# One attention-and-FFN decode step on one core: a TensorE loop over one pair of batches instead of two, with V copied to a fixed place

## The chip, the core and the metric

The kernel runs on one core of one Trainium2 chip. Five engines work side by side, each on its own instruction stream, and meet only at semaphores: TensorE (PE in the profile) multiplies matrices and writes to the accumulator banks (PSUM), VectorE (DVE) and ScalarE (ACT) read those banks and write to on-chip memory (SBUF), GpSimd (POOL) fills and copies SBUF, SyncE (SP) starts nearly all transfers. Transfers from main memory are carried out by 16 DMA engines that all transfers share. The metric is device time in microseconds (us) for one execution; lower is better.

## What is computed

One new token for each of four batches goes through layer normalisation, and its result through two branches whose outputs are added to the input: attention over a window of 4096 cached positions (32 query heads, 8 kv heads, head size 128) and a SwiGLU FFN of width 1792. Cut to what matters:

```python
x = A_x                                   # (4, 1, 512)
xn = _layernorm(x, axis=-1)
def _A_ref(x, k_cache, v_cache, wq, wo):  # caches (4, 8, 16384, 128)
    q = (x @ wq).reshape(B, 1, 32, 128).transpose(0, 2, 1, 3)
    k = jnp.repeat(k_cache[:, :, Sk - W:, :], 4, axis=1)   # W = 4096
    v = jnp.repeat(v_cache[:, :, Sk - W:, :], 4, axis=1)
    p = _softmax(jnp.einsum("bhqd,bhkd->bhqk", q, k) * (128 ** -0.5), axis=-1)
    o = jnp.einsum("bhqk,bhkd->bhqd", p, v)
    return o.transpose(0, 2, 1, 3).reshape(B, 1, 32 * 128) @ wo
def _B_ref(x, w_gate, w_up, w_down):
    return (_silu(x @ w_gate) * (x @ w_up)) @ w_down
return x + _A_ref(xn, ...) + _B_ref(xn, ...)
```

Everything is bf16 in memory. The K and V windows are 64 MB of the 81 MB that are read.

## The kernel before

**The unit of work** is a turn: one kv head of two batches. There are ND = 16 of them. A turn's K is one load of 2048 KB to `KB[128, 8192]`, its V one load to `VB`, each with two buffers; positions and the two batches lie on the 128 partitions, so a mask takes out the scores of the wrong batch. A turn is cut in halves of 32 blocks of 128 positions.

**What happens to a turn's data**: TensorE transposes 32 blocks of K (`transposes`, line 397) into four accumulator banks of 8 blocks each (groups g = 0 to 3), the four banks are copied to `KT` in SBUF (`evac`, L311, all by VectorE), and 32 score matmuls (`scores`, through the helper at L369) multiply `KT` by the queries of the turn; then the same for the second half. Scores of both halves fill one bank `ps_S`. VectorE takes their maximum along the free axis (`row_max`, L316), TensorE turns it over the partitions (`max_rows`), VectorE reduces it and makes a diagonal `Dg` (`shift`, L321 to L323), TensorE subtracts it from all scores by a matmul (`shift`), ScalarE takes exp into `P` (L282). Then TensorE sums the denominators (4 matmuls with `ones`) and multiplies `P` by V (`pv`, 32 matmuls a half), and VectorE normalises into `OT` (`norm`, L327 to L331).

**Order.** The stages of neighbouring turns overlap. TensorE's stream is written by hand: in each pass of its loop (L445) two turns, b = 0 and 1, and in each turn d: transposes of the first half, maximum of the scores of d - 1, second half of PV of d - 2, mask and scores of the first half, shift of d - 1, transposes of the second half, denominators and first half of PV of d - 1, scores of the second half. For this the scores have two banks, `P` two halves, and the queries of the turn are read from `QZ` at an address taken from a register (`QF[:, ds(...)]`), since one pass of the loop names only b. Every wait is a `wait_ge` on a semaphore, in a loop against a value computed from the loop register.

**Transfers** are started by SP in the order of its stream: WQ at the start, then K of turns 0 and 1, gate and up weights, V of turn 0, then K(d) and V(d - 1) by turns; the down weights stand before the last V, and the five pieces of WO at the end. K(d) waits until K(d - 2) has been transposed, V(d) until the PV of d - 2 is done.

**Around the loop**: layer normalisation and the query projection before it, with `QZ` filled at L302; after it the gate and up projections (from L466), the last PV, the down projection, four transposes of `OT`, a regrouping, and the rows of WO (`out_rows`, L193), then y and its store. ScalarE loads its function table three times: before L273, L277 (square root) and L282 (exp).

Of the kernel before, what the change touches and what calls it, by code (L numbers as in the profile page):

```python
# [5 lines left out]
BF16 = mybir.dt.bfloat16  # L6
FP32 = mybir.dt.float32
# [5 lines left out]
def bass_parallel_sum__sliding_block_cached__swiglu_ffn__decode_kernel(  # L13
# [72 lines left out]
    OT = sb("oT", [128, B, REP + HQ], BF16)  # L86
# [13 lines left out]
    ps_S = [ps("ps_s%d" % s, [128, 512], FP32) for s in range(2)]  # L100
# [8 lines left out]
    mt_ps = ps_acc[0:C, 0:128]  # L109
# [29 lines left out]
    s_tr = sem("s_tr")  # L139
    s_ev = sem("s_ev")  # L140
# [28 lines left out]
    def kv_ap(cache, d, fold):  # L169
        b0 = d % 2 * 2  # L170
        return cache[b0:b0 + 2, d // 2, Sk - W:, :].rearrange("b (q t) d -> q b (t d)", t=fold * NT)
# [13 lines left out]
    def load_kv(eng, buf, cache, d):  # L185
        return load(eng, buf[:, d % 2 * KVN:(d % 2 + 1) * KVN], kv_ap(cache, d, 1), kv_ap(cache, d, FOLD))
# [10 lines left out]
    with nc.Block() as block:  # L197

        @block.gpsimd
        def _(eng):  # L200
# [32 lines left out]
            eng.memset(VB[:, HKN:].bitcast(FP32), 0.0)  # L233
            eng.drain()
            eng.engine_nop().then_inc(s_const, 1)
            eng.engine_nop().then_inc(d_v[1], 16)
# [33 lines left out]
        def _(eng):  # L270
# [9 lines left out]
            for d in range(-1, ND):  # L280
                eng.wait_ge(s_sh, d + 2)
                eng.activation(P[:, d % 2 * PS:d % 2 * PS + SN], ps_S[d % 2][:], ACT.Exp, scale=SCALE).then_inc(s_p, 1)  # L282
# [4 lines left out]
        def _(eng):  # L287
# [13 lines left out]
            for i in range(2):  # L301
                last = eng.tensor_copy(  # L302
                    QZ[:].rearrange("p (k i) c -> p k i c", i=2)[:, :, i, 0:C].rearrange("p k (m h) -> p k m h", m=2),
                    qT.rearrange("p (k h x) -> p k x h", h=REP, x=32)[:, :, 2 * i:2 * i + 2, :])
            last.then_inc(s_qz, 1)
            eng.engine_nop().then_inc(s_ev, NG)

            def evac(u, tr):
                for g in range(NG):
                    eng.wait_ge(s_tr, tr + g + 1)  # L310
                    eng.tensor_copy(KT[:, u * HKN + 1024 * g:u * HKN + 1024 * (g + 1)],  # L311
                                    kt_ps[g].rearrange("p a b -> p (a b)")).then_inc(s_ev, 1)

            def row_max(bank, n):
                eng.wait_ge(s_sc, n)
                eng.tensor_reduce(RM[:], ps_S[bank][:].rearrange("p (t c) -> p c t", c=C), AX.X,  # L316
                                  ALU.max).then_inc(s_rm, 1)

            def shift(n):
                eng.wait_ge(s_mt, n)  # L320
                eng.tensor_reduce(m8[:], mt_ps, AX.X, ALU.max)  # L321
                eng.drain()
                eng.tensor_scalar(Dg[:], I8[:], m8[:, 0:1], -1.0, ALU.mult, ALU.mult).then_inc(s_dg, 1)  # L323

            def norm(n, b, r):
# [5 lines left out]
                eng.tensor_tensor(OT[:, 2 * b:2 * b + 2, ds(r * REP, REP)],  # L331
                                  O_ps.rearrange("p (j h) -> p j h", j=2),
                                  den[:].rearrange("p (j h) -> p j h", j=2), ALU.mult).then_inc(s_nrm, 1)

            with eng.Fori(0, ND // 2) as r:
                for b in range(2):
                    row_max(1 - b, 2 * r + (b + 1))
                    evac(0, 4 * NG * r + 2 * NG * b)
                    shift(2 * r + (b + 1))
                    norm(2 * r + (b + 1), b, r)  # L340
                    evac(1, 4 * NG * r + (2 * NG * b + NG))
            row_max(1, ND + 1)
            shift(ND + 1)
            norm(ND + 1, 0, ND // 2)

# [13 lines left out]
            norm(ND + 2, 1, ND // 2)  # L359

# [6 lines left out]
        def _(eng):  # L367
# [20 lines left out]
            def mask(bank):  # L388
                return mm(ps_S[bank][:].rearrange("p (t c) -> p t c", c=C), mkr[:],
                          mkc[:].rearrange("j (o c) -> j o c", o=1).to_broadcast([2, NT, C]), start=True)  # L390

            def transposes(s, ev, b):
                for g in range(NG):
                    eng.wait_ge(s_ev, ev + g + 1)
                    for k in range(8):
                        a = b * KVN + s * HKN + 128 * (8 * g + k)
                        last = eng.transpose(kt_ps[g][:, k, :], KB[:, a:a + 128], ident[:])  # L397
                    last.then_inc(s_tr, 1)

            def scores(s, ev, b, q):  # L400
                if s == 0:
                    mask(b)
                eng.wait_ge(s_ev, ev + 2 * NG)
                for t in range(HT):
                    o = C * (s * HT + t)
                    n = min(WIDE, SN - o)
                    last = mm(ps_S[b][:, o:o + n], KT[:, s * HKN + 128 * t:s * HKN + 128 * (t + 1)], q(n))
                if s == 1:
                    last.then_inc(s_sc, 1)
# [131 lines left out]
```

## Time and profile before

| | us |
|---|---|
| three runs | 197.21, 196.9, 195.21 |
| median | 196.9 |
| span of the profiled execution | 194.3 |
| TensorE matmul, busy in the span | 164.1 |
| TensorE weight load, busy | 142.1 |
| VectorE, busy | 115.4 |
| ScalarE, busy | 17.0 |
| GpSimd, busy | 10.5 |
| read from main memory | 81.01 MB, 417 GB/s over the span |

The span runs from the first to the last instruction of one execution that the hardware profiler recorded; the device time of a run also has what lies around it, here 196.9 - 194.3 = 2.6 us by the median. In lines of a timeline the first number is the start in us from the span's start, the second the duration of the whole group, then engine, source line, operation, output <- input, and the number of instructions; brackets give the idle time of the engine before it and what ended it. In lines of a group the numbers behind the bar are busy us and mean ns of one instruction. In the chain of waits each line is start, duration and what the end of the kernel was waiting for at that time. A line that starts with SPq or ACTq is the start of a transfer.

### The profile page before, as it was taken

The page shows a single profiled execution, that of the slowest core. Times are in us where ns is not written, and L with a number is a line of the kernel's source. Part 1 is how long each engine was busy: PE and PEld are TensorE (multiplying, and loading weights), DVE is VectorE, ACT ScalarE, POOL GpSimd, SP SyncE. Part 2 cuts the span into 40 slices and gives each one's busy share as a digit, 9 for nine tenths or more (in the row PEclk, how much of TensorE's full clock was granted, in tenths as well). Part 3 has the DMA queues.
Part 4 walks back from the last instruction along what each step waited for, and adds up shares of the span by engine and source line. Part 5 has one row for each costly group of instructions (what it writes and reads, how often), then busy time and mean ns, then how long its engine had stood idle before and what let it go on. Part 6 is the DMA issues. An engine that isn't in the chain of part 4 may idle for free.

```text
span 194.3 us, 7749 instructions
## 1 busy us (share of the span) xinstructions
PE 164.1 (84%) x3460; PEld 142.1 (73%) x3461; DVE 115.4 (59%) x250; ACT 17.0 (9%) x27; POOL 10.5 (5%) x23
## 2 busy tenths in 40 slices
PE   0127999949999989898989898989898989898894
PEld 0112988848989878888878887888887888887662
DVE  1004757617677767676767676767676767675530
ACT  5700010100110101010101010101010101010100
POOL 8930000000000000000000000000000000000000
PEclk9999999988999999999999999999999999999999
DMA  6999997999999999999999999999999999999992
GB/s 217 432 432 432 511 452 332 432 437 432 425 432 425 432 432 432 438 445 432 432 432 432 438 432 438 432 438 432 432 432 432 445 432 432 432 428 428 401 400 94
DMA packets 3589, 81.09 MB, mean 417 GB/s; under 512 B 664, under 2 KB 800, under 8 KB 1184
## 3 DMA queue, kind: packets, MB, share of 16 engines
q1 hardware_dynamic: 3568, 81.01, 97.3%
q8 instruction: 4, 0.07, 0.1%
q10 hardware_dynamic: 16, 0.01, 0.0%
q14 instruction: 1, 0.01, 0.0%
HBM read 81.01 MB, written 0.00 MB: 417 GB/s over the span
## 4 chain that ended last, share of the span: by engine, by line
DMA 61%; PE 34%; issue 1%; DVE 1%; SPq 1%; DVEq 0%
DMA kbuf<-in_A_k_cache_dram 46%; PE ps_kt L397 18%; DMA wo_sb<-in_A_wo_dram 9%; PE ps_s L369 8%; DMA wq_sb<-in_A_wq_dram 6%; PE ps_o L369 5%; PE ps_kt L369 2%; PE ps_acc L369 1%; PE ps_acc L193 1%; DVE kT L311 1%; SPq L251 1%; DVE kT L299 0%; SPq L177 0%; DVE y_sb L507 0%; DVE qz L302 0%
## 5 line engine op out<-in xcount | busy, mean ns | idle before, releaser
L311 DVE COPY kT<-ps_kt 128x1024 bf16<-128x1024 bf16 x128 | 79.9, 683 | 27.4 <-PE ps_kt L397 27.3
L397 PE MATMUL ps_kt<-ident,kbuf 128*128 128x128 bf16 x1024 | 65.7, 225 | 10.4 <-DMA kbuf<-in_A_k_cache_dram 10.4
L397 PEld LDWEIGHTS ps_kt<-ident,kbuf 128*128 128x128 bf16 x1024 | 60.1, 101 | 15.8 <-issue 15.8
L369 PE MATMUL ps_o<-p,vbuf 128*128 128x64 bf16 x1120 | 39.2, 195 | 0.0
L369 PEld LDWEIGHTS ps_o<-p,vbuf 128*128 128x128 bf16 x1120 | 36.0, 99 | 1.2
L369 PEld LDWEIGHTS ps_s<-qz,kT 128*128 128x128 bf16 x1024 | 31.4, 98 | 6.7 <-issue 3.7
L369 PE MATMUL ps_s<-qz,kT 128*128 x1024 | 34.7, 192 | 1.2
L282 ACT ACTIVATE p<-ps_s 128x512 bf16<-128x512 f32 x17 | 10.2, 597 | 161.9 <-PE ps_s L369 161.9
L316 DVE TENSOR_REDUCE rm<-ps_s 128x8 bf16<-128x512 f32 x17 | 11.8, 691 | 19.8 <-PE ps_s L369 19.8
L369 PE MATMUL ps_o<-p,ones 128*128 128x128 bf16 (+1 forms) x69 | 7.0, 222 | 2.3 <-DVE qz L302 1.3
L369 PE MATMUL ps_kt<-wq_sb,xnT 128*32 128x512 bf16 x32 | 3.6, 629 | 5.3 <-DMA wq_sb<-in_A_wq_dram 5.3
L369 PEld LDWEIGHTS ps_o<-p,ones 128*128 128x128 bf16 x69 | 4.5, 98 | 3.5 <-issue 2.2
L369 PE MATMUL ps_s<-mkc,mkr 2*128 2x512 bf16 x17 | 6.9, 404 | 0.0
L374 PE MATMUL ps_acc<-i,xn 4*128 4x4 f32 x4 | 0.6, 254 | 7.4 <-ACT xn L279 7.4
L369 PE MATMUL ps_s<-dg,ones 8*128 8x512 bf16 x17 | 6.5, 385 | 0.0
L327 DVE TENSOR_REDUCE den<-ps_o 128x8 f32<-128x128 f32 x18 | 5.0, 275 | 2.5 <-PE ps_o L369 2.5
L369 PEld LDWEIGHTS ps_kt<-wq_sb,xnT 128*32 128x32 bf16 x32 | 1.2, 138 | 6.8 <-issue 6.8
L299 DVE STREAM_TRANSPOSE kT<-ps_kt 128x512 f32<-128x512 f32 x2 | 1.4, 717 | 8.0 <-PE ps_kt L369 8.0
L374 PEld LDWEIGHTS ps_acc<-i,xn 4*128 4x128 f32 x4 | 0.6, 207 | 7.3 <-issue 7.3
L233 POOL MEMSET vbuf<- 128x6144 f32 x1 | 5.2, 5222 | 0.0
L321 DVE TENSOR_REDUCE m<-ps_acc 8x1 f32<-8x128 f32 x17 | 4.6, 270 | 0.3 <-PE ps_acc L369 0.3
L331 DVE TENSOR_TENSOR oT<-ps_o,den 128x8 f32 (+1 forms) x18 | 3.0, 166 | 2.9 <-issue 2.7
(68 smaller groups left out, 48.6 us busy)
## 6 DMA issues: line engine op xcount, KB each, us to landing
kbuf<-in_A_k_cache_dram SPq DMA_DIRECT2D x16, 2048.0 KB, 12.5
vbuf<-in_A_v_cache_dram SPq DMA_DIRECT2D x16, 2048.0 KB, 11.2
wq_sb<-in_A_wq_dram SPq DMA_DIRECT2D x1, 4096.0 KB, 12.3
wo_sb<-in_A_wo_dram SPq DMA_DIRECT2D x1, 2048.0 KB, 14.9
wg_sb<-in_B_w_gate_dram SPq DMA_DIRECT2D x1, 1792.0 KB, 24.2
wu_sb<-in_B_w_up_dram SPq DMA_DIRECT2D x1, 1792.0 KB, 27.6
wd_sb<-in_B_w_down_dram SPq DMA_DIRECT2D x1, 1792.0 KB, 14.9
wo_sb<-in_A_wo_dram SPq DMA_DIRECT2D x1, 896.0 KB, 17.8
```

Source lines behind the costliest of these rows:

```text
L193: last = eng.matmul(ps_acc[64 * n:64 * n + B, 0:256], OP[:, c, :], WO[:, c, 256 * n:256 * n + 256], start=False, stop=True, skip_group_che ...
L233: eng.memset(VB[:, HKN:].bitcast(FP32), 0.0)
L251: eng.dma_start(WO[:, a:b, :], wo_ap[:, a:b, :]).then_inc(d_wo[n], 16)
L282: eng.activation(P[:, d % 2 * PS:d % 2 * PS + SN], ps_S[d % 2][:], ACT.Exp, scale=SCALE).then_inc(s_p, 1)
L299: eng.transpose(qT[:, 512 * n:512 * n + 512], ps_kt[n][:])
L311: eng.tensor_copy(KT[:, u * HKN + 1024 * g:u * HKN + 1024 * (g + 1)], kt_ps[g].rearrange("p a b -> p (a b)")).then_inc(s_ev, 1)
L316: eng.tensor_reduce(RM[:], ps_S[bank][:].rearrange("p (t c) -> p c t", c=C), AX.X, ALU.max).then_inc(s_rm, 1)
L321: eng.tensor_reduce(m8[:], mt_ps, AX.X, ALU.max)
L327: eng.tensor_reduce(den[:], den_ps.rearrange("p (t c) -> p c t", c=C), AX.X, ALU.add)
L331: eng.tensor_tensor(OT[:, 2 * b:2 * b + 2, ds(r * REP, REP)], O_ps.rearrange("p (j h) -> p j h", j=2), den[:].rearrange("p (j h) -> p j h" ...
L369: return eng.matmul(o, l, r, start=start, stop=stop, skip_group_check=True)
L397: last = eng.transpose(kt_ps[g][:, k, :], KB[:, a:a + 128], ident[:])
```

## The change

TensorE's loop now covers one turn, with static addresses, and everything that differed between turns is brought to one place:

- **V** is copied by VectorE from its buffer to `VS`, the last 8192 columns of the query weights' place, the second half of the old turn's V early in a turn and the first half of the new one's late. PV reads `VS`. V's buffer is free when its second half has been copied, and V(d) waits for that.
- **Queries**: GpSimd copies the turn's queries from `QZ` to a slot `QS`. GpSimd also waits for the landing of K and V and tells the others by `s_k` and `s_v`.
- **One score bank** and one `P`. The mask of the new scores waits until exp has read the old ones. The maximum's matmul gets a bank of its own, `ps_mt`.
- **TensorE's stream**: maximum of the last scores, transposes of the first half, shift, transposes of the second half, mask, scores of the first half, denominators, first half of PV, scores of the second half, second half of PV; the PV of a turn follows its scores by one turn. K still has two buffers, so the two transposes are written twice (`pe_even`, `pe_odd`), the rest once (`pe_both`), with branches between. The branch with a hint at the old end is gone.
- **Evacuation**: VectorE copies groups 0 and 2 of `KT`, ScalarE groups 1 and 3, exp between the halves.
- **Transfers**: K and V alternate from the start; gate, up and down weights and WO come after the last V.
- Turns run head by head over one pair of batches and then the other, and `OT` is laid out to fit.

The diff, cut to its core:

```diff
-    P = sb("p", [128, 2 * PS], BF16)
+    VS = WQ[:, NC * HQ * Dh - KVN:NC * HQ * Dh]
+    P = sb("p", [128, PS], BF16)
+    QS = sb("qs", [128, WIDE], BF16)
-    ps_S = [ps("ps_s%d" % s, [128, 512], FP32) for s in range(2)]
+    ps_S = ps("ps_s", [128, 512], FP32)
+    ps_mt = ps("ps_mt", [128, 512], FP32)
...
+    def at(d):
+        return (d + 1) % 2 * KVN
...
         @block.gpsimd
...
+            eng.wait_ge(s_qz, 1)
+            for d in range(ND):
+                eng.wait_ge(d_k[d % 2], 16 * (d // 2 + 1))
+                eng.engine_nop().then_inc(s_k, 1)
+                if d:
+                    eng.wait_ge(s_sc, d)
+                eng.tensor_copy(QS[:], QZ[:, d, :]).then_inc(s_qs, 1)
+                eng.wait_ge(d_v[d % 2], 16 * (d // 2 + 1))
+                eng.engine_nop().then_inc(s_v, 1)
...
         @block.sync
...
                 if d >= 2:
-                    eng.wait_ge(s_tr, 2 * NG * (d - 1))
+                    eng.wait_ge(s_t[1][NG - 1], d - 1)
...
-                eng.wait_ge(s_pv, d + 1)
+                if d >= 1:
+                    eng.wait_ge(s_vs[1], d)
...
-            load_k(0)
-            load_k(1)
+            for d in range(ND):
+                load_k(d)
+                load_v(d)
             load(eng, WG[:], wg_ap, fold_rows(B_w_gate)).then_inc(d_wg, 16)
             load(eng, WU[:], wu_ap, fold_rows(B_w_up)).then_inc(d_wu, 16)
-            load_v(0)
-            for d in range(2, ND):
-                load_k(d)
-                load_v(d - 1)
             load(eng, WD[:], wd_ap, fold_rows(B_w_down)).then_inc(d_wd, 16)
-            load_v(ND - 1)
...
         @block.scalar
...
-            for d in range(-1, ND):
-                eng.wait_ge(s_sh, d + 2)
-                eng.activation(P[:, d % 2 * PS:d % 2 * PS + SN], ps_S[d % 2][:], ACT.Exp, scale=SCALE).then_inc(s_p, 1)
+            with eng.Fori(1, ND + 2) as r:
+                for h in range(2):
+                    for g in (1, 3):
+                        eng.wait_ge(s_t[h][g], r)
+                        eng.activation(KT[:, h * HKN + 1024 * g:h * HKN + 1024 * (g + 1)],
+                                       kt_ps[g].rearrange("p a b -> p (a b)"), ACT.Copy).then_inc(s_e[h][g], 1)
+                    if h == 0:
+                        eng.wait_ge(s_sh, r)
+                        eng.activation(P[:, 0:SN], ps_S[:], ACT.Exp, scale=SCALE).then_inc(s_p, 1)
...
         @block.vector
...
+            with eng.Fori(1, ND + 2) as r:
+                here = eng.snap((r % 2) * KVN, min_val=0, max_val=KVN)
+                other = eng.snap(((r + 1) % 2) * KVN, min_val=0, max_val=KVN)
+                eng.wait_ge(s_mt, r)
+                eng.tensor_reduce(m8[:], mt_ps, AX.X, ALU.max)
+                eng.drain()
+                eng.tensor_scalar(Dg[:], I8[:], m8[:, 0:1], -1.0, ALU.mult, ALU.mult).then_inc(s_dg, 1)
+                norm(r)
+                for h in range(2):
+                    for g in (0, 2):
+                        eng.wait_ge(s_t[h][g], r)
+                        eng.tensor_copy(KT[:, h * HKN + 1024 * g:h * HKN + 1024 * (g + 1)],
+                                        kt_ps[g].rearrange("p a b -> p (a b)")).then_inc(s_e[h][g], 1)
+                eng.tensor_copy(VS[:, HKN:], VB[:, ds(other + HKN, HKN)]).then_inc(s_vs[1], 1)
+                eng.wait_ge(s_v, r)
+                eng.wait_ge(s_pv0, r)
+                eng.tensor_copy(VS[:, 0:HKN], VB[:, ds(here, HKN)]).then_inc(s_vs[0], 1)
+                eng.wait_ge(s_sc, r)
+                eng.tensor_reduce(RM[:], ps_S[:].rearrange("p (t c) -> p c t", c=C), AX.X, ALU.max).then_inc(s_rm, 1)
+            norm(ND + 2)
...
         @block.tensor
...
+            def turn(d):
+                r = eng.snap(count, min_val=1, max_val=ND + 1)
+                eng.wait_ge(s_rm, r)
+                mm(mt_ps, RM[:], ident[:], start=True).then_inc(s_mt, 1)
+                eng.wait_ge(s_k, r)
+                transposes(0, r, d)
+                eng.wait_ge(s_dg, r)
+                mm(St, ones[0:C, :], Dg[:].rearrange("j (o c) -> j o c", o=1).to_broadcast([C, NT, C])).then_inc(s_sh, 1)
+                transposes(1, r, d)
+
+            eng.br("pe_even")
+            with nc.body("pe_even", valid_engines=PE):
+                turn(0)
+                eng.br("pe_both")
+            with nc.body("pe_both", valid_engines=PE):
+                r = eng.snap(count, min_val=1, max_val=ND + 1)
+                eng.wait_ge(s_p, r)
+                mask()
+                eng.wait_ge(s_qs, r)
+                scores(0)
+                eng.wait_ge(s_nrm, r)
+                for j in range(SN // 128):
+                    mm(den_ps, ones[:], P[:, 128 * j:128 * (j + 1)], start=(j == 0))
+                eng.wait_ge(s_vs[0], r)
+                pv(0).then_inc(s_pv0, 1)
+                for g in range(NG):
+                    eng.wait_ge(s_e[1][g], r)
+                scores(1).then_inc(s_sc, 1)
+                eng.reg_alu(count, count, 1, ALU.add)
+                eng.reg_alu(odd, 1, odd, ALU.subtract)
+                eng.wait_ge(s_vs[1], r)
+                pv(1).then_inc(s_pv, 1)
+                eng.br_lt(odd, 1, on_true="pe_even", on_false="pe_more")
+            with nc.body("pe_more", valid_engines=PE):
+                eng.br_lt(count, ND + 2, on_true="pe_odd", on_false="pe_done")
+            with nc.body("pe_odd", valid_engines=PE):
+                turn(1)
+                eng.br("pe_both")
+            nc.switch_bb("pe_done")
...
-            eng.br_lt(flag, 1, on_true="tensor_tail", on_false="tensor_never")
-            with nc.body("tensor_never", valid_engines=[mybir.EngineType.PE]):
-                eng.br_lt(flag, 1, on_true="tensor_never", on_false="tensor_tail").branch_hint(hint)
-            nc.switch_bb("tensor_tail")
```

In the tail, the down projection now follows the transposes of `OT`, and the last PV and normalisation stand inside the loop's last turn.

More of the change, by code (lines that the diff above doesn't have):

```diff
@@ L108, in bass_parallel_sum__sliding_block_cached__swiglu_ffn__decode_kernel @@
     xT_ps = ps_acc[:, 0:NC * B]
[L109 removed]
+    mt_ps = ps_mt[0:C, 0:128]
     gate_ps = ps_kt[0][:, 0:NF * 32]
@@ L386, in _, with mask @@
                 last.then_inc(s_q, 1)
[L388 to L392, printed above, removed]
+            St = ps_S[:].rearrange("p (t c) -> p t c", c=C)
+            def mask():
+                return mm(St, mkr[:], mkc[:].rearrange("j (o c) -> j o c", o=1).to_broadcast([2, NT, C]), start=True)
@@ L411, in max_rows @@
[L411 to L433 removed]
+                    last = mm(ps_S[:, o:o + n], KT[:, h * HKN + 128 * t:h * HKN + 128 * (t + 1)], QS[:, 0:n])
@@ L481, in _ @@
                     mm(ps_acc[64 * n:64 * n + B, 0:256], guT[:, t, :], WD[:, t, 256 * n:256 * n + 256])
-            eng.wait_ge(s_nrm, ND + 2)
-            for i in range(B):
-                last = eng.transpose(
-                    tr_ps[:, i, :],
-                    OT[:, i, REP:], ident[:])
-            last.then_inc(s_t4, 1)
             spin(2)
```

141 lines of the change are left out of this document (46 added, 95 removed).

## The prediction

> **What bounds the kernel now.** I read the slices of the page first, then the chain that ended last, then the timeline of one turn (one batch pair and one kv head: K transposed, scores, exp, PV), last the DMA by stretch.
>
> ```profile
> PE   0127999949999989898989898989898989898894
> DMA  6999997999999999999999999999999999999992
> ```
>
> Two resources look full. The chain of waits tells which one ends last:
>
> ```profile
> 0.80 12.35 DMA wq_sb<-in_A_wq_dram
> ...
> 28.36 14.14 DMA kbuf<-in_A_k_cache_dram
> ...
> 78.42 12.51 DMA kbuf<-in_A_k_cache_dram
> ...
> 97.79 12.52 DMA kbuf<-in_A_k_cache_dram
> ...
> 155.97 12.52 DMA kbuf<-in_A_k_cache_dram
> ...
> 173.47 17.78 DMA wo_sb<-in_A_wo_dram
> 191.25 0.04 issue
> 191.30 1.30 PE ps_acc L193 x20
> 192.60 0.02 issue
> 192.62 0.41 DVE y_sb L507
> ```
>
> K loads land at 78.42 + 12.51 = 90.93 and two turns later at 97.79 + 12.52 = 110.31: 19.38 us for two K and two V loads, so 9.69 us a turn, 4.85 us a load of 2048 KB.
>
> ```profile
> kbuf<-in_A_k_cache_dram SPq DMA_DIRECT2D x16, 2048.0 KB, 12.5
> wq_sb<-in_A_wq_dram SPq DMA_DIRECT2D x1, 4096.0 KB, 12.3
> wg_sb<-in_B_w_gate_dram SPq DMA_DIRECT2D x1, 1792.0 KB, 24.2
> ```
>
> At that rate a 1792 KB load takes 4.24. From WQ's landing (13.15) to K2's (28.36 + 14.14 = 42.50) there are four loads of 2048 KB and two of 1792 KB, 27.9 us of work in 29.35: 1.5 us are lost early. From 42.50 to K15 (168.49) it is 126.0 us for 26 loads, 4.85 each: nothing is lost. So the DMA is the bound from 42.5 on, and no order of the same bytes ends sooner, but for the 1.5 us. The turn itself:
>
> ```profile
> 91.05 1.96 PE L397 MATMUL ps_kt<-ident,kbuf 128*128 128x128 bf16 x32 [0.68 <-DMA kbuf<-in_A_k_cache_dram]
> 91.70 2.48 DVE L311 COPY kT<-ps_kt 128x1024 bf16<-128x1024 bf16 x4 [0.60 <-PE ps_kt L397]
> ...
> 94.10 0.27 DVE L321 TENSOR_REDUCE m<-ps_acc 8x1 f32<-8x128 f32 x1
> 94.22 0.54 SPq L177 DMA_DIRECT2D vbuf<-in_A_v_cache_dram  x1
> ...
> 95.30 0.17 DVE L331 TENSOR_TENSOR oT<-ps_o,den 128x8 f32 x1 [0.17 <-issue]
> 95.48 0.39 PE L369 MATMUL ps_s<-dg,ones 8*128 8x512 bf16 x1
> ...
> 99.00 1.06 PE L369 MATMUL ps_s<-qz,kT 128*128 x32
> 100.10 0.69 DVE L316 TENSOR_REDUCE rm<-ps_s 128x8 bf16<-128x512 f32 x1 [1.16 <-PE ps_s L369]
> 100.75 1.96 PE L397 MATMUL ps_kt<-ident,kbuf 128*128 128x128 bf16 x32 [0.69 <-DMA kbuf<-in_A_k_cache_dram]
> ```
>
> TensorE works 9.70 - 0.68 = 9.0 us of a turn and waits 0.7 for K. That is its whole room.
>
> **The change, part by part.**
>
> *TensorE.* The matmuls of a turn are the same in number and shape (64 transposes, 64 scores, 64 PV, 4 denominators, mask, shift, maximum), so 9.0 us stay. The static query slot can only save issue gaps; worth nothing while K is waited for. The branches are sequencer work behind queued PV matmuls; that cover gone, see the branch rival.
>
> *One score bank.* The mask now waits for exp. From the first transpose, t0: transposes to 1.96, shift to about 2.3, second half to about 4.1. ScalarE first copies groups 1 and 3. No row shows that copy:
>
> ```profile
> L282 ACT ACTIVATE p<-ps_s 128x512 bf16<-128x512 f32 x17 | 10.2, 597 | 161.9 <-PE ps_s L369 161.9
> L284 ACT ACTIVATE ex<-wq_sb 128x56 f32<-128x56 f32 x1 | 0.2, 248 | 1.0 <-DVE wq_sb L347 1.0
> L282 ACT ACT_TABLE_LOAD x1 | 1.3, 1283 | 0.0
> ```
>
> The slope (597 - 248)/456 is 0.77 ns an element, so 1024 elements cost 597 + 512 x 0.77 = 0.99 us; between 0.60 (the row itself) and 1.19 (twice it). Group 3 is copied at 1.96 + 0.99 = 2.95, exp ends at 3.55, before the second half does (4.1): hidden, with 0.5 to spare.
>
> *V copied.* VectorE loses four evacuations of 0.62 (2.48/4) and gains two copies of 4096 elements, SBUF to SBUF, which no row shows. Upper end: four of the evacuation copies, same elements, 2.48. Lower end: the smallest SBUF operation,
>
> ```profile
> L351 DVE TENSOR_SCALAR ex<-ex 128x56 f32<-128x56 f32 x1 | 0.1, 148 | 0.0
> ```
>
> 0.15. I take the middle, 1.3: the upper row reads PSUM, and the lower is all fixed cost. The Trainium skill, "VectorE: DVE Perf Modes", section "The perf-mode tier table (the rule you actually need)", gives a bf16 SBUF copy of 2048 elements 693 ns and caps any copy from PSUM at half that rate; twice 693 would be 1.39, an estimate by which the sum is the same; no run here shows it yet.
>
> VectorE's turn: row maximum 0.69, wait for the maximum matmul about 0.3, then 94.10 to 95.47 (1.37) for shift and normalisation, evacuations 4 x 0.62, two issue gaps of 0.17, and two copies c: 5.2 + 2c. With c = 1.3 it is 7.8 and fits in 9.69; with c = 2.48 it is 10.2 and does not; it decides from c = 2.25. The row maximum stands behind the second copy, which starts with scores(1): it begins c rather than 1.10 us (99.00 to 100.10) after them, 0.2 late, inside the 0.7.
>
> *V's loads.* Before, V was issued 94.22 - 91.05 = 3.2 us after t0. Now it waits for the copy of the old second half: after the third group of the second transposes (about 3.6), 0.62, 0.17 and 1.3: t0 + 5.7. The next K is queued behind it on SP. Two loads are queued at t0, 9.69 us; WQ's 4096 KB took 12.35 for 9.69 of transfer, so 2.66 us lie around a transfer, and the issue must come by t0 + 7.0. It holds, with 1.3 to spare.
>
> *The first turn is different.*
>
> ```profile
> 19.05 3.59 PE L397 MATMUL ps_kt<-ident,kbuf 128*128 128x128 bf16 x32
> ...
> 22.77 1.89 PE L369 MATMUL ps_o<-p,vbuf 128*128 128x64 bf16 x32
> ...
> 25.01 1.11 PE L369 MATMUL ps_s<-qz,kT 128*128 x32
> ```
>
> Its 32 transposes took 3.59, not 1.96, and PV 1.89 against the later 1.11 of 32 equal-sized matmuls: the array is slow until about 24.7. WQ, K0, V0, K1 now lie ahead, so K1 lands at 13.15 + 3 x 4.85 = 27.7, and V1 must be issued by 25.0. The maximum goes first (19.25), transposes end at 22.8, shift 23.2, then 1.5 us at the slow pace (13 transposes) and 19 at 0.06: 25.8, third group evacuated at 26.2, copied at 27.65. V1 is 2.6 us late, K2 stands behind it, and the DMA idles. Later turns have V in time, so it is paid once. Against it stands the early loss of 1.5, which can fall into this idle time: +1.1 to +2.6. I take +1.7, a little under the middle, since 2.66 contains the first transfer's start-up.
>
> *POOL.* K's and V's landing reaches TensorE and VectorE by way of POOL, and it copies the query.
>
> ```profile
> L228 POOL MEMSET xnT<- 128x64 f32 x1 | 0.1, 141 | 0.0
> ```
>
> About 0.14 for 64 elements, needed 4 us later; the hop delays t0 by some 0.1, which the 1.3 covers.
>
> *Weights last.* Bytes are equal. K15 lands at 13.15 + 31 x 4.85 + 1.7 = 165.2, two turns end at 183, and the way from there to the out rows, of which before has
>
> ```profile
> 179.91 0.94 PE L369 MATMUL ps_kt<-wg_sb,xnT 128*32 128x448 bf16 x16
> ...
> 188.01 2.57 PE L193 MATMUL ps_acc<-wo_sb,oP 128*4 128x256 bf16 x44 [0.21 <-DVE oP L364]
> ```
>
> 8.1 + 2.6 us with the last pair's PV (about 2.2) in it, takes some 9: 192, against a landing at 191.25 + 1.7 = 192.95. Hidden by 1.
>
> The sum: 194.3 + 1.7 = 196.0 of span. What lies around it is 196.9 - 194.3 = 2.6 by the median, kept: **198.6 us**.
>
> **The rivals.**
>
> *No gap.* The first turn warms sooner, or the idle time swallows the early loss and more of the 1.5. Then the time is 196.9 - 1.5 to + 0.5, 196.2 in the middle. For it: the loss exists. Against: 2.6 us of lateness has four steps behind it. Chance 0.15.
>
> *VectorE becomes the bound* (the slower side). At c = 2.48 its turn is 10.2, 0.5 over, and up to 1.0 over where it also waits for the second transposes: 16 x 0.5 to 1.0 is 8 to 16, less the 1.3 of lead: 205 to 212 with the first-turn gap. For it: the only COPY rows run at that rate. Chance 0.11.
>
> *ScalarE reloads its table every turn.* Before, exp's load stands once, ahead of 17 exps; in the new loop a copy precedes exp in a body that is entered with the square root's table. A load of 1.28 between group 3 and exp puts exp's end at 4.83, 0.7 to 0.8 after the second transposes; the turn is 9.8, and 9.9 with slower copies: 16 x 0.1 to 0.3 and the lost lead, about 201, up to 204. Placed ahead of the turn's first copy it costs nothing. Chance 0.18.
>
> *The branches stall.* TensorE jumps back once a turn, once in two turns before. If each jump had to fetch code, the nearest price is a small load: X's, issued at 0.80 and used at 2.56.
>
> ```profile
> 0.80 0.55 ACTq L271 DMA_DIRECT2D x_sb<-in_A_x_dram  x1
> ...
> 2.56 0.67 DVE L289 TENSOR_REDUCE st_neg<-x_sb 4x1 f32<-4x512 bf16 x1 [2.56 <-DMA x_sb<-in_A_x_dram]
> ```
>
> 1.76 less the 0.7 of room, 16 times: 17 us, 215. Against it stands the DMA between 45 and 180, seven passes of a loop twice as long:
>
> ```profile
> DMA packets 2203, 58.36 MB, mean 432 GB/s; under 512 B 446, under 2 KB 446, under 8 KB 446
> ## 3 DMA queue, kind: packets, MB, share of 16 engines
> q1 hardware_dynamic: 2203, 58.36, 100.3%
> ```
>
> Not one instruction packet. The Trainium skill, "Runtime: NRT & Kernel Launch", section "Instruction fetch mechanics", holds that a taken branch whose target lies outside a window of two blocks must wait for a fetch; by that rule the old loop too would fetch in every pass, and this trace does not agree. Chance 0.04.
>
> **How the numbers follow.** My case, DMA-bound with one gap, has 0.52. One per cent is 1.97 us, about what a measurement of this kernel can tell from no change. Of my case (+0.5 to +3) some 0.29 lies within it and 0.23 above; of the no-gap case 0.10 within and 0.05 faster; of the table case 0.03 within and 0.15 slower; the other two, 0.15, are slower. So faster 0.05, same 0.42, slower 0.53: the likeliest case straddles the line, and its own range is 197.4 to 199.9. The whole range must reach the table case and the near end of VectorE's: 196.0 to 206.0, with about 0.07 below and 0.11 above left out.
>
> **What would show it.** Right: GB/s of 430 in all slices but one near 27 to 30, K's waits of about 0.5 us on the transposes in every turn, the V copy at 1.1 to 1.5, V issued under 6 us after t0. Wrong: a VectorE copy over 2; table loads x17 standing between copies and exp; instruction packets by the dozen; no K waits at all, with idle DMA slices all along; or a DMA that does not idle near 28.

## The result: slower by 3.9%, and the profile after

| | before | after |
|---|---|---|
| median of four runs (us) | 196.08 | 204.37 |
| lowest and highest | 195.21, 197.21 | 202.22, 205.64 |
| span of the profiled execution | 194.3 | 200.7 |

The ratio is 1.0386, with an interval from 1.0296 to 1.0476. One run of the new kernel (205.64) and the profiled executions of e2 and e6 below were over 1.5% slower than the fastest run of the same kernel; the ratios leave such runs out, no trace of e2 is read here, and of e6 only the late turns. The forecast of 198.6 had the sign and its range holds the time, but the likeliest case's own range, 197.4 to 199.9, does not: the loss is 8.3 us by the medians of the table, 7.6 by the ratio and 6.4 by the two profiled spans (the new kernel's profile is of its fastest run, 202.22), where 1.7 were expected.

The slices of the kernel after, on the page of its profile:

```profile
PE   0137999698979797979796999797979797999875
...
PEclk9999999999999999999999699999999999999999
DMA  6999989999999999999999989999999999999892
GB/s 242 451 444 431 418 317 421 425 485 405 431 333 457 385 438 418 444 372 431 392 425 438 444 333 451 418 411 425 418 385 425 411 431 425 425 491 423 359 399 82
```

The DMA row is as full as before, yet the GB/s row is not: slices of 333, 385, 372 and 392 stand among those of 430, from 55 us to 120. The engines count as busy and move less. The chain of waits of the kernel after shows where:

```profile
35.46 13.79 DMA kbuf<-in_A_k_cache_dram
49.36 1.96 PE ps_kt L416 x32
51.64 1.46 PE ps_kt L416 x24
53.73 1.23 DVE wq_sb L357
54.98 0.54 SPq L188
55.56 13.89 DMA kbuf<-in_A_k_cache_dram
...
95.86 13.95 DMA kbuf<-in_A_k_cache_dram
109.92 3.25 PE ps_kt L416 x32
...
146.88 13.44 DMA kbuf<-in_A_k_cache_dram
...
169.66 27.97 DMA wo_sb<-in_A_wo_dram
197.68 1.27 PE ps_acc L204 x20
```

In the kernel before, the chain also came back to a landing of K every two turns, by way of TensorE and the start of the next K, but V had been started earlier and each two turns took 19.38 us. Here the ring is another: K lands, its transposes, the V copy of L357, the start of V, the start of K behind it, K lands. K landed at 35.46 + 13.79 = 49.25 and eleven turns later at 146.88 + 13.44 = 160.32: 10.10 us a turn where the kernel before took 9.69. The first transpose, t0, is 0.11 after the landing. One turn of the timeline:

```profile
49.36 1.96 PE L416 MATMUL ps_kt<-ident,kbuf 128*128 128x128 bf16 x32 [0.61 <-POOLq L253]
...
52.29 0.60 ACT L309 ACTIVATE p<-ps_s 128x512 bf16<-128x512 f32 x1
...
53.47 0.39 PE L386 MATMUL ps_s<-mkc,mkr 2*128 2x512 bf16 x1
53.73 1.22 DVE L357 COPY wq_sb<-vbuf 128x4096 bf16 x1
...
54.75 1.28 ACT L305 ACT_TABLE_LOAD   x1
...
54.98 0.54 SPq L188 DMA_DIRECT2D vbuf<-in_A_v_cache_dram  x1
55.56 0.60 SPq L188 DMA_DIRECT2D kbuf<-in_A_k_cache_dram  x1
```

V is issued 54.98 - 49.36 = 5.62 us after t0, where 5.7 was forecast, and the K behind it lands 69.45 - 54.98 = 14.47 after that issue. The two terms make two turns, 20.1 us. So the change did to V's start what the prediction said; the deadline for it was not t0 + 7.0.

### The profile page after: what moved, and what is told of

Its sections match the earlier page's. It is cut to its first block, busy times and chain, and to the rows that moved or that the text cites. A ratio compares the mean times of both kernels' runs of the same rounds, so it can differ in the third digit from the quotient of the medians.

```text
span 200.7 us, 7999 instructions
## 1 busy us (share of the span) xinstructions
PE 164.9 (82%) x3557; PEld 142.8 (71%) x3558; DVE 121.3 (60%) x224; ACT 100.1 (50%) x111; POOL 10.4 (5%) x40
## 4 chain that ended last, share of the span: by engine, by line
DMA 61%; PE 24%; DVE 7%; SPq 3%; issue 3%; DVEq 0%; POOLq 0%
DMA kbuf<-in_A_k_cache_dram 41%; PE ps_kt L416 17%; DMA wo_sb<-in_A_wo_dram 14%; DMA wq_sb<-in_A_wq_dram 6%; DVE wq_sb L357 4%; PE ps_s L386 3%; SPq L188 3%; PE ps_kt L386 2%; PE ps_o L386 1%; DVE wq_sb L360 1%; DVE rm L362 1%; PE ps_acc L204 1%; DVE kT L355 1%; SPq L276 1%; DVE kT L326 0%
## 5 line engine op out<-in xcount | busy, mean ns | idle before, releaser
L305 ACT ACTIVATE kT<-ps_kt 128x1024 bf16<-128x1024 bf16 x68 | 66.5, 1035 | 82.7 <-PE ps_kt L416 82.7
L416 PE MATMUL ps_kt<-ident,kbuf 128*128 128x128 bf16 x1088 | 69.1, 224 | 12.7 <-POOLq L253 12.7
L355 DVE COPY kT<-ps_kt 128x1024 bf16<-128x1024 bf16 x68 | 46.7, 690 | 20.6 <-PE ps_kt L416 20.4
L386 PE MATMUL ps_o<-p,wq_sb 128*128 128x64 bf16 x1088 | 37.3, 193 | 0.0
L386 PE MATMUL ps_s<-qs,kT 128*128 128x64 bf16 (+3 forms) x1088 | 36.7, 191 | 0.0
L386 PEld LDWEIGHTS ps_s<-qs,kT 128*128 128x128 bf16 x1088 | 33.5, 98 | 3.9 <-issue 3.9
L360 DVE COPY wq_sb<-vbuf 128x4096 bf16 x17 | 20.9, 1227 | 23.3 <-PE ps_o L386 23.3
L386 PEld LDWEIGHTS ps_o<-p,wq_sb 128*128 128x128 bf16 x1088 | 34.4, 98 | 0.0
L357 DVE COPY wq_sb<-vbuf 128x4096 bf16 x17 | 20.7, 1216 | 0.0
L256 POOL COPY qs<-qz 128x64 bf16<-128x64 bf16 x16 | 3.8, 237 | 158.9 <-DMA kbuf<-in_A_k_cache_dram 148.6
L348 DVE TENSOR_REDUCE m<-ps_mt 8x1 f32<-8x128 f32 x17 | 4.7, 279 | 6.3 <-PE ps_mt L386 6.3
L386 PE MATMUL ps_mt<-ident,rm 128*8 128x128 bf16 x17 | 3.8, 222 | 5.0 <-DVE rm L362 5.0
## 6 DMA issues: line engine op xcount, KB each, us to landing
wg_sb<-in_B_w_gate_dram SPq DMA_DIRECT2D x1, 1792.0 KB, 12.7
```

What stands on the lines that cost most here:

```text
L256: eng.tensor_copy(QS[:], QZ[:, d, :]).then_inc(s_qs, 1)
L305: eng.activation(KT[:, h * HKN + 1024 * g:h * HKN + 1024 * (g + 1)], kt_ps[g].rearrange("p a b -> p (a b)"), ACT.Copy).then_inc(s_e[h][g], 1)
L355: eng.tensor_copy(KT[:, h * HKN + 1024 * g:h * HKN + 1024 * (g + 1)], kt_ps[g].rearrange("p a b -> p (a b)")).then_inc(s_e[h][g], 1)
L357: eng.tensor_copy(VS[:, HKN:], VB[:, ds(other + HKN, HKN)]).then_inc(s_vs[1], 1)
L360: eng.tensor_copy(VS[:, 0:HKN], VB[:, ds(here, HKN)]).then_inc(s_vs[0], 1)
L386: return eng.matmul(o, l, r, start=start, stop=stop, skip_group_check=True)
```

## The experiments

The medians of the kernel before, run beside them on the same chip, are 195.43 us (e1 to e4) and 195.44 (e5 to e8, and e10); e9 is a single run. Times of issue are counted from K's landing here, 0.11 before t0: 5.73 for the kernel after.

### e1: the old half of V copied earlier

```diff
                 for h in range(2):
                     for g in (0, 2):
...
+                    if h == 0:
+                        eng.tensor_copy(VS[:, HKN:], VB[:, ds(other + HKN, HKN)]).then_inc(s_vs[1], 1)
-                eng.tensor_copy(VS[:, HKN:], VB[:, ds(other + HKN, HKN)]).then_inc(s_vs[1], 1)
```

> The new kernel with one VectorE instruction moved: the copy of V's second half stands before the second half's two evacuations instead of behind them, so V is issued some 3.7 us after the turn's first transpose instead of 5.6. Same bytes, same copies. Lead theory (V's load starts too late for the transfer queue; two turns take the 5.6 us to V's issue plus 14.5 us from there to the landing of the K behind it, 20.1 instead of 19.4): 3.7 + 14.5 = 18.2 is under 19.4, the transfers set the pace again, K lands every 9.7 us, about 5 us fewer: 198 to 200 us. Contention theory (the two copies of 4096 elements a turn slow the transfers by their traffic): as many copies as before, 203 to 205 us.

Measured: 196.53, ratio to before 1.0055 (1.0038 to 1.0072). Nearly the whole loss is gone, with the same work on every engine and in every transfer. A turn in its timeline:

```profile
77.35 1.96 PE L417 MATMUL ps_kt<-ident,kbuf 128*128 128x128 bf16 x32 [0.64 <-POOLq L253]
...
79.51 1.22 DVE L358 COPY wq_sb<-vbuf 128x4096 bf16 x1
...
80.75 0.54 SPq L188 DMA_DIRECT2D vbuf<-in_A_v_cache_dram  x1
...
87.04 1.96 PE L417 MATMUL ps_kt<-ident,kbuf 128*128 128x128 bf16 x32 [0.64 <-POOLq L253]
```

V is issued 3.40 us after t0, the next turn begins after 9.69, and the copy itself still takes 1.22. So neither the copies nor TensorE's new loop cost the time; the late place of that one copy, ahead of V's start, does.

### e2: K ahead of V on SP

```diff
-            for d in range(ND):
-                load_k(d)
-                load_v(d)
+            load_k(0)
+            load_v(0)
+            load_k(1)
+            for d in range(1, ND):
+                if d + 1 < ND:
+                    load_k(d + 1)
+                load_v(d)
```

> The new kernel with K(r+1) issued ahead of V(r) on SP; all else as it is. K is then issued about 4.4 us after the turn's first transpose and V 5.7. Lead theory: the queue is fed earlier, but V now lands a load later than the turn that copies it needs it; V's landing, then copy 1.2, row maximum 0.7 and the hops come before the next turn: 4.4 + 14.5 + 2.6 = 21.5 us for two turns, some 10 us slower than the new kernel, 210 to 215 us. A theory in which only the early feeding of the queue counts: faster, 198 to 200. Contention theory: 203 to 205.

Measured: 209.37, ratio 1.0656 (1.0605 to 1.0708). K can be issued sooner than V, so one might expect this order to keep the queue fed; it loses 5 us more. The interval of the lead theory was missed by 0.6 on its fast side; why the order loses is argued in the expectation, and not shown by a trace.

### e3: no table loads in the loop

```diff
+            eng.activation(st_var[:], st_std[:], ACT.Exp)
             with eng.Fori(1, ND + 2) as r:
```

> The new kernel with one exp on a single column ahead of ScalarE's loop, so that the loop is entered with exp's table and the load of 1.28 us in each of the 17 turns goes. Lead theory: the load runs behind the turn's last copy, beside nothing that waits: no change, 203 to 205 us. Table theory (ScalarE's turn is lengthened): 2 to 6 us faster.

Measured: 204.73, ratio 1.045 (1.0401 to 1.0498): no gain. The 17 loads of 1.28 us in the kernel after stand at the end of ScalarE's turn (54.75 above), when exp has long ended; in e3's trace the loop has none.

### e4: the old kernel with a later V

The kernel before, with nothing of the change but a later start of V: it also waits for exp.

```diff
                 eng.wait_ge(s_pv, d + 1)
+                eng.wait_ge(s_p, d + 1)
                 load_kv(eng, VB, A_v_cache, d)
```

> The old kernel with one wait more on SP: V is issued only after the exp of the turn, about 5.5 us after the turn's first transpose instead of 3.2. No copy of V, no branch, no table load. Lead theory: 5.5 + 14.5 = 20.0 us for two turns instead of 19.4, 13 to 15 turns: 3.5 to 5 us slower than the old kernel, 199.5 to 201 us. Contention theory and every theory that blames work that the new kernel adds: unchanged, 195 to 197 us.

Measured: 202.71, ratio 1.0351 (1.0312 to 1.0389). Two turns of SP in its timeline:

```profile
98.11 0.54 SPq L177 DMA_DIRECT2D vbuf<-in_A_v_cache_dram  x1
99.33 0.54 SPq L177 DMA_DIRECT2D kbuf<-in_A_k_cache_dram  x1
107.82 0.54 SPq L177 DMA_DIRECT2D vbuf<-in_A_v_cache_dram  x1
109.03 0.54 SPq L177 DMA_DIRECT2D kbuf<-in_A_k_cache_dram  x1
```

K had landed at 92.46 and 102.16, so V is issued 5.65 us after K's landing, and K lands every 10.02 us on average from K2 (42.45) to K15 (172.72). No V copy, no branches of a new loop, no new query slot: with the start of V came a loss whose interval overlaps that of the change. It was larger than expected, and the copies' traffic as a cause falls.

### e5 and e6: the start of V moved later and a little earlier

e5 lets V also wait for the first half of the new PV; e6 puts the copy between VectorE's two evacuations of the second half.

```diff
                     eng.wait_ge(s_vs[1], d)
+                    eng.wait_ge(s_pv0, d)
```

```diff
                     for g in (0, 2):
+                        if (h, g) == (1, 0):
+                            eng.tensor_copy(VS[:, HKN:], VB[:, ds(other + HKN, HKN)]).then_inc(s_vs[1], 1)
...
-                eng.tensor_copy(VS[:, HKN:], VB[:, ds(other + HKN, HKN)]).then_inc(s_vs[1], 1)
```

> V's load also waits for the first half of the new PV, which puts its issue at about t0 + 6.8 instead of t0 + 5.6. Lead theory (the K that is issued behind V lands 14.5 us after V's issue, and that is two turns): (6.8 + 14.5) / 2 = 10.65 us a turn instead of 10.05, and over 14 turns +8.4 on 204.4: 210 to 215. Rival, a fixed price for each turn in which the queue has run dry, whenever V comes: 203 to 206.

> The copy of the old second half stands between VectorE's two evacuations of the second half, so V is issued at about t0 + 4.8. Lead theory: a turn stays at 9.69 as long as V is issued by 2 x 9.69 - 14.5 = t0 + 4.9, so this is at the edge and costs almost nothing: 196.5 to 198.5. Rival, a loss that grows evenly from no loss at t0 + 3.5 to 8 us at t0 + 5.6: 8 x 1.3 / 2.1 = 5 us, 200.5 to 202.5.

Measured: e5 208.8, ratio 1.0686 (1.0646 to 1.0727); e6 197.41, ratio 1.0087 (1.0058 to 1.0117). Of the chains of waits, first e5, then e6:

```profile
78.87 14.18 DMA kbuf<-in_A_k_cache_dram
...
151.75 14.11 DMA kbuf<-in_A_k_cache_dram
```

```profile
85.74 13.96 DMA kbuf<-in_A_k_cache_dram
...
143.89 13.98 DMA kbuf<-in_A_k_cache_dram
```

In e5 K landed at 93.05 and seven turns later at 165.86, 10.40 a turn, with V issued 6.88 after the landing in most turns; 10.65 were expected and the time lies 1.2 under the interval. In e6 six turns took 157.87 - 99.70 = 58.17, 9.70 each, with V issued at 4.84. So nothing is lost at 4.84, and 0.35 to 0.4 a turn at 5.73. The loss begins somewhere between them, and then grows with the delay: by 0.3 a turn for the 1.15 us from 5.73 to 6.88.

### e7: only the first V late

The change's order in the first turn, the early copy in all others: the prediction's mechanism alone. VectorE's first turn stands ahead of its loop.

```diff
...
-            with eng.Fori(1, ND + 2) as r:
...
+            def dve_turn(r, early):
...
+                    if h == 0 and early:
+                        eng.tensor_copy(VS[:, HKN:], VB[:, ds(other + HKN, HKN)]).then_inc(s_vs[1], 1)
+                if not early:
+                    eng.tensor_copy(VS[:, HKN:], VB[:, ds(other + HKN, HKN)]).then_inc(s_vs[1], 1)
...
+            dve_turn(1, False)
+            with eng.Fori(2, ND + 2) as r:
+                dve_turn(r, True)
```

> The old second half's copy is early in every turn but the first, which keeps the order of the change: the prediction's mechanism alone. The prediction's own size for it is +1.7 on 196.5: 198.2. The packets say less: K2 landed at 39.58 with the late first V and 38.51 without, and the last weights are waited for less than the tail's own work: +0.3 to +1.1, 196.8 to 197.6. Rival, one late start that stays in the queue and is paid again in every turn: 200 or more.

Measured: 197.83, ratio 1.0097 (1.0066 to 1.0129), 1.3 above e1. It is paid once, not in every turn: from K2 to K15, K lands every 9.69 us. What the first turn has of the 1.3 stays open: in the profiled run V(1) was issued at 24.02, sooner than the 25.90 of the kernel after, K2 landed 0.2 later than in e1 (38.73 against 38.51), and the rest came in the tail, where the granted clock was 0.68 between 185 and 190. That clock does not account for the median: the runs of 197.79, 197.87 and 197.92 had a mean granted clock of 1.0. The expected interval, 196.8 to 197.6, was missed by 0.2.

### e9: the loads alone

All arithmetic is left out; V(d) and K(d+1) are issued a set time after K(d-1) landed. VectorE measures that time by copies within SBUF, 5 of 2048 elements a turn in the first column below and one more in each further column.

```diff
...
+                for _ in range(COPIES[d]):
+                    eng.drain()
+                    last = eng.tensor_copy(KT[:, 4096:6144], KT[:, 0:2048])
+                last.then_inc(s_go, 1)
...
+                eng.wait_ge(s_go, d + 1)
+                load_kv2(eng, VB, A_v_cache, d + 1).then_inc(d_v[(d + 1) % 2], 16)
+                load_kv2(eng, KB, A_k_cache, d + 2).then_inc(d_k[d % 2], 16)
```

> All arithmetic is left out (the output is a copy of X): only loads of the kernel's K and V run, in the order of the loop, V(d) and K(d+1) issued a set time after the landing of K(d - 1), 6 turns for each of seven times between about 3.5 and 9 us; then 5 loads of V alone, 5 pairs of V and K and 3 loads of WQ, each started when nothing else is under way. The prediction's lead (2.66 us around a transfer) gives 9.69 a turn up to 7.0 us, a V alone 7.5, a pair 12.35. If the lead lies in the transfers themselves, a turn grows from about 5 us on, by half of what V is later (10.05 at 5.7, 10.5 to 10.7 at 7), and a pair that starts from nothing takes 14 to 14.5. Rival, the busy engines draw out the transfers of the change: alone the prediction's figures hold, 9.69 at 5.7 and a pair at 12.35.

| V issued after K's landing (us) | 3.95 | 4.71 | 5.48 | 6.25 | 7.02 | 7.78 | 8.55 |
|---|---|---|---|---|---|---|---|
| a turn, half of K(d-1)'s landing to K(d+1)'s | 9.83 | 9.69 | 10.18 | 10.59 | 10.95 | 11.05 | 10.80 |

(Means over the six turns. In the first column four of six are 9.69 and two are 10.1; in the later ones single turns scatter, from 10.41 to 11.32 in the sixth and from 10.49 to 11.02 in the seventh. The last V of a column comes up to 0.4 late in four of them.) Rows of its chain of waits that belong to the second and the fifth column:

```profile
103.14 14.11 DMA kbuf<-in_A_k_cache_dram
...
122.54 14.09 DMA kbuf<-in_A_k_cache_dram
...
269.11 14.28 DMA kbuf<-in_A_k_cache_dram
...
290.98 14.57 DMA kbuf<-in_A_k_cache_dram
```

Landings at 117.25 and 136.63 are two turns of 9.69 apart; those at 283.39 and 305.55, two turns of 11.08. No engine but VectorE was at work, and its 6 copies a turn in the second column, more elements than the change copies, cost nothing. So contention with the engines' work falls. But the lead theory falls too in the form it had until here, a transfer that takes 4.8 us longer than its bytes, as the pairs started from nothing show:

```profile
508.85 0.53 SPq L188 DMA_DIRECT2D vbuf<-in_A_v_cache_dram  x1
...
521.26 0.54 SPq L188 DMA_DIRECT2D vbuf<-in_A_v_cache_dram  x1
...
533.56 0.54 SPq L188 DMA_DIRECT2D vbuf<-in_A_v_cache_dram  x1
...
546.00 0.54 SPq L188 DMA_DIRECT2D vbuf<-in_A_v_cache_dram  x1
```

A pair takes 12.3 to 12.4 us, as the prediction's 9.69 + 2.66 has it, and not 14 to 14.5. A single V took 7.5. So the 2.66 is right for a load that finds the queue empty. What fails is that work still in the queue hides it. At 7.02 the queue still holds 9.69 - 7.02 = 2.67 us of work, which should hide all of the 2.66, and at 7.78 it holds 1.91; but two turns took 2 x 10.95 - 19.38 = 2.52 and 2 x 11.05 - 19.38 = 2.72 too long, about the whole 2.66. At 8.55 the prediction's rule would give (8.55 + 12.35) / 2 = 10.45, and 10.80 were measured; whether a turn really gets shorter again from 7.78 to 8.55 is not shown, the scatter being as large.

The records of single packets show where the time goes. A load is 64 packets of 32 KB, four on each of the 16 DMA engines, 1.21 us each. The records do not name the engine or the load; joined by end and start, which leaves a join open by some hundredths, three of the sixteen chains in the kernel after show this, in us after K's landing at 59.34 (V issued at 5.73):

```
            last packets of K          idle   first packet of V
chain 1     4.50  5.71  6.92 to 8.13   0.57   8.70, 2.74 long, to 11.45
chain 2     4.60  5.81  7.02 to 8.23   0.33   8.57, 2.80 long, to 11.37
chain 3     4.89  6.10  7.31  8.53     none   9.74, 1.21 long, to 10.95
```

Chain 3 is at the pace of the landing, 9.69 after it. Chains 1 and 2 run 1.5 to 1.6 us ahead. They are empty at 8.1 to 8.2, V's data begins on them 2.8 to 3.0 us after the issue, and their first packet takes 2.8 us in place of 1.21. They fall 2 us back, from first to last: their four packets of V end at 15.0 to 15.1, and V lands at 15.40. In other turns other chains fall back. In the Trainium skill, "DMA: Bandwidth & Descriptors", section "Why a DMA increments its semaphore by 16 and not by 1", a transfer runs on up to 16 engines that finish independently while the semaphore counts them; the trace agrees, with the last packets of this K ending between 8.13 and 9.74.

The same records count the damage. 32 KB packets over 1.7 us long, between 85 and 160 us of each trace:

| before | after | e1 | e4 | e5 | e10 |
|---|---|---|---|---|---|
| 0 of 991 | 34 of 943 | 0 of 990 | 23 of 964 | 57 of 908 | 0 of 470 (K alone) |

The 34 long packets of the kernel after took up to 2.80 us and all began 1.3 to 3.4 us after an issue of V. For 15 of them all sixteen engines had a packet on record 0.06 us before, so a gap like those of chains 1 and 2 is not needed: a packet that begins so soon after V's issue can be long whether its engine stood idle or not. Why it is long is not shown; a long packet counts as busy, which is why the DMA row stays full.

### e10: V in two halves

This was made from that reading: nothing on VectorE is moved, but half of V's bytes are in the queue before the fast engines run out.

```diff
...
-                if d >= 1:
-                    eng.wait_ge(s_vs[1], d)
-                load_kv(eng, VB, A_v_cache, d).then_inc(d_v[d % 2], 16)
+                for h in range(2):
+                    if d >= 1:
+                        eng.wait_ge(s_vs[h], d)
+                    eng.dma_start(VB[:, at(d) + h * HKN:at(d) + (h + 1) * HKN],
+                                  kv_ap(A_v_cache, d, 1)[:, :, h * HKN:(h + 1) * HKN]).then_inc(d_v[d % 2], 16)
```

> VectorE's order is left as the change has it; V is loaded in two halves of columns, and the first half is issued as soon as that half of the old V has been copied, at the end of the turn before; only the second half waits for the late copy. If the loss is engines that run dry between t0 + 8 and the arrival of V's transfers, 2.4 us more work in the queue covers it: 9.69 a turn, 196.3 to 198, like the early copy. Against it, a transfer in pieces of 8 KB may run slower than in 32 KB, which no run shows: then up to 201, with full slices. Rival, the copy's place on VectorE itself costs the time: 203 to 205.

Measured: 197.24, ratio 1.0092 (1.0075 to 1.0109). From SP's timeline:

```profile
93.36 0.54 SPq L273 DMA_DIRECT2D vbuf<-in_A_v_cache_dram  x1
93.94 0.61 SPq L188 DMA_DIRECT2D kbuf<-in_A_k_cache_dram  x1
```

The issue at 93.36, 5.72 after K's landing at 87.64, is that of the second half; the first half of that V was issued at 86.20. K lands every 9.74 us, with the late copy in its place. So it is the work left in the queue that decides, and not VectorE's order as such. V's packets are smaller here, 8 KB that took 0.31 us each, none longer; whether that helps as well, e10 alone can't tell, but e1 and e6 lose nothing in their turns with the packets of the change.

### e8: the early copy with a shorter tail

e1's chain of waits ends on TensorE: its last 20 matmuls wait for no transfer. In e8 ScalarE copies the transposed and the regrouped output, and the regrouping stands ahead of the down projection, without the idle matmuls between.

```diff
...
+            eng.wait_ge(s_t4, 1)
+            eng.activation(OB[:], tr_ps, ACT.Copy).then_inc(s_ob, 1)
+            eng.wait_ge(s_pm, 1)
+            eng.activation(OP[:].rearrange("p c b -> p b c"), op_ps.rearrange("p (b c) -> p b c", b=B), ACT.Copy).then_inc(s_op, 1)
...
-            eng.wait_ge(s_guT, 1)
-            eng.wait_ge(d_wd, 16)
...
-            spin(2)
             eng.wait_ge(s_ob, 1)
...
             last.then_inc(s_pm, 1)
-            spin(1)
+            eng.wait_ge(s_guT, 1)
+            eng.wait_ge(d_wd, 16)
...
             eng.wait_ge(s_op, 1)
```

> The early copy of the V that is left, and in the tail ScalarE copies the transposed output and the regrouped output, and the regrouping stands before the down projection, so that the rows of WO need not wait for it. If the last 1.1 us of the early copy's kernel over the kernel before are the tail's own work (its last 20 matmuls begin 0.75 us after the weights that they wait for landed): 195.6 to 196.0. Rival, they are the transfers or lie around the span: 196.4 to 196.7.

Measured: 195.67, ratio 1.0021 (0.9999 to 1.0042). The ends of the timelines, first e1, then e8:

```profile
188.82 2.57 PE L204 MATMUL ps_acc<-wo_sb,oP 128*4 128x256 bf16 x44 [0.21 <-DVE oP L382]
...
191.69 1.26 PE L204 MATMUL ps_acc<-wo_sb,oP 128*4 128x256 bf16 x20 [0.31 <-PEq L208]
```

```profile
187.44 2.57 PE L204 MATMUL ps_acc<-wo_sb,oP 128*4 128x256 bf16 x44
...
191.39 1.26 PE L204 MATMUL ps_acc<-wo_sb,oP 128*4 128x256 bf16 x20 [1.38 <-DMA wo_sb<-in_A_wo_dram]
```

The rows of WO begin 1.4 us sooner and TensorE waits for the weights again. The kernel is level with the one before, which moves the same bytes; no version here beats it.

## Why the prediction was right in sign and wrong in size

**What held.** The transfers are the bound. That the range holds the time is luck: its upper part stood for the table loads and the slow VectorE, and neither cost the time. The copy of V took 1.22 us (forecast 1.3). Twice the figure for 2048 elements in the Trainium skill, "VectorE: DVE Perf Modes", section "The perf-mode tier table (the rule you actually need)", gave 1.39, an estimate that came out 0.17 high. ScalarE's copies took 1.04 (0.99), and exp ended at 52.89, before the mask of the new scores at 53.47: one score bank is hidden. The rows of the kernel after:

```profile
L305 ACT ACTIVATE kT<-ps_kt 128x1024 bf16<-128x1024 bf16 x68 | 66.5, 1035 | 82.7 <-PE ps_kt L416 82.7
L416 PE MATMUL ps_kt<-ident,kbuf 128*128 128x128 bf16 x1088 | 69.1, 224 | 12.7 <-POOLq L253 12.7
...
L305 ACT ACT_TABLE_LOAD x17 | 21.8, 1283 | 0.3
L357 DVE COPY wq_sb<-vbuf 128x4096 bf16 x17 | 20.7, 1216 | 0.0
```

TensorE's wait for K, by way of POOL, is 12.7 us in 13 waits, 1.0 a turn instead of 0.5 to 0.7: its own work still fits, and it is the one who waits.

**The step that failed** is this: "Two loads are queued at t0, 9.69 us; WQ's 4096 KB took 12.35 for 9.69 of transfer, so 2.66 us lie around a transfer, and the issue must come by t0 + 7.0. It holds, with 1.3 to spare." The 2.66 is right for an empty queue (e9: pairs of 12.3 to 12.4), but work still queued does not hide it as the sum has it: alone, with V at 7.02 after the landing, 2.52 of it was paid. The 9.69 is right only for the slowest of 16 engines: t0 is its time, and in the kernel after the fastest had about 8.1. From there 2.8 to 3.0 us go off until V's data begins, so the limit lies near 5.2 after the landing for the turn shown, an estimate that stands between the 4.84 of e6 that cost nothing and the 5.73 of the change. Past it the price is also higher than the gap, since packets that begin so soon after the issue took up to 2.8 us. A margin of 1.3 was a shortfall of about half a microsecond, in every turn.

**The sum.** Against e1, whose transfers run without loss from K2 on, the landings of the kernel after are 1.07 us late at K2 (39.58 to 38.51), the first turn; 4.52 more at K15 (170.07 to 164.48), 0.35 a turn over 13 turns, the term that was missing; and 1.09 more at the last weights (198.56 to 191.88). TensorE's tail is better hidden behind them, by 0.69. Together 5.99, and the spans differ by 6.0. This is the fastest run of the new kernel; its others took 1.4 us and more longer, and no trace shows where.

**The first turn** was priced at 1.7 and is worth about 1.1 in this execution: the first transposes took 3.12 and not 3.59, so V was issued at 25.90 instead of 27.65. In the profiled execution of e3, whose first turn on TensorE and VectorE is the same, they took 3.59, V was issued at 27.30 and K2 landed at 40.97, 2.5 after e1's: the term varies between executions, and 1.7 lies between the two. That it is paid once is as forecast, but what followed it was not quiet.

**Weights last** is hidden by 0.7 in the kernel after (TensorE's last 20 matmuls wait for WO), a little less than the 1 forecast; with the loop at full pace, as in e1, it is not, and e8 shows what the tail then costs: 0.9 us of median.

**The rivals.** No gap: refuted. VectorE as the bound: refuted by its 1.22, and it waited 20.4 us in all for the transposes. Table loads: there are 17, as that rival said, but where they cost nothing (e3). Branches: instruction packets number three in one queue and one in another, for the whole execution. None of the rivals was the missing term: a V whose margin is not there was forecast for the first turn alone. Two of the rivals' sums are slightly off, with no bearing on the outcome: 198.6 + 8 to 16 - 1.3 is 205.3 to 213.3 and not 205 to 212, and the middle of 195.4 to 197.4 is 196.4 and not 196.2.

**The signs.** V under 6 us after t0, a copy of 1.1 to 1.5 and waits for K came true, and said nothing against the sum. The one sign that failed, GB/s of 430 in all slices but one, was the one that points at the step.

## What to carry to other kernels

Do not take the deadline of a refill from the landing plus the bytes still queued: the landing belongs to the slowest of 16 engines, and here a load issued with 4.85 us of work still queued ahead of it lost nothing, while one with 3.96 left lost 0.35 us a turn. The operation that frees a buffer belongs as early in its engine's stream as its inputs allow, ahead of work with slack: one copy moved ahead of two others brought the ratio from 1.0386 down to 1.0055. Read the GB/s row beside the DMA row: a full DMA row hid the whole loss.

## What had not been expected of the hardware

A load that came slightly late paid as much as one that found the queue empty: alone, with V issued 7.02 after the landing and 2.67 us of work still queued, two turns were 2.52 us too long, and a pair that started from nothing was 2.66 longer than its bytes. Where packets take 1.21 us, some that began 1.3 to 3.4 us after V's issue took up to 2.8, with a gap before them or without.

A slow stretch of TensorE delays the next loads: near 110 us the granted clock of the kernel after fell below 0.7 for a slice, its first transposes took 3.25 us (109.92 in the chain of waits) in place of 1.96, and V left 7.27 and 6.60 us after K's landing in that turn and the next, instead of 5.73. Whether TensorE's waits for K brought the clock down is not shown.
